# Attention scores computed with the keys on partitions, the maximum taken from the product of the high parts, and x normalised at the end

## The chip, the cores and the metric

One core of one Trainium2 chip runs the whole program. The metric is the device time in microseconds of one execution; shorter is better. The kernel before took 1103.06 us (median of three runs, 1101.69 to 1104.33).

## The reference

Attention in which a key counts for a query only if both fall into the same hash bucket, followed by a feed-forward layer with a squared ReLU. Everything is float32.

```python
batch, n_heads, seq, head_dim = (4, 8, 768, 64)       # B, H, S, D
n_tokens, d_model, d_ff = (3072, 512, 2048)
...
q_bits = (np.einsum('bhsd,dk->bhsk', q, proj) > 0)      # 6 bits; k_bits likewise
mask = q_bucket[:, :, :, None] == k_bucket[:, :, None, :]
scores = np.where(mask, (1 / np.sqrt(D)) * (q @ k.transpose(0, 1, 3, 2)), -1e9)
attn = np.exp(scores - scores.max(-1, keepdims=True))
attn = attn / (attn.sum(-1, keepdims=True) + 1e-9)
x = (attn @ v).transpose(0, 2, 1, 3).reshape(B * S, H * D)
r = np.maximum(x @ w_in, 0.0)
return (s * (r * r) + b) @ w_out
```

A query without any key in its bucket has equal scores everywhere, so its row of x is the mean of v.

## The kernel before

**Slots.** The work is cut into slots: 256 queries (`CH`) of one head of one batch, 96 in all. Batch 0 goes first with chunk 0 of its eight heads (slots 0 to 7), then the other two chunks of each head (8 to 23); the batches 1 to 3 follow with three chunks a head (24 to 95). Two neighbouring heads share a tile of x (64 partitions each), so the chunks of an odd head finish a pair.

**Precision.** A product of float32 numbers is made from fast `float32r` matmuls: an operand is split into a high part (rounded to `float32r`) and a low part (what is left). The first eight slots, and the values of some heads of batch 0 (`PLAIN`), use plain float32 matmuls, which take four passes.

**Scores** (`weights`, lines 467 to 503). Queries lie on partitions: for 128 queries two products (lines 483 and 484) add up scores and mask, 768 keys wide, in two banks of PSUM. The mask is part of the product: the bits stand as 12 more rows of the operands, times large constants. DVE takes the row maximum (491), ScalarE the exponential with the sum as a second output (492), DVE makes the inverse of the sum in four operations on one column (498 to 501), and POOL multiplies the 768 weights by it and puts equal weights into rows without a key (503).

**Values** (`values`, lines 508 to 571). The product with v needs the weights with keys on partitions, so PE transposes them (530), twelve 128 x 128 blocks a slot. ScalarE copies each group of four out of PSUM as the high part (541), DVE subtracts to get the low part (542), and PE multiplies both with v's two parts (551, 552). The result x is split again (568, 569) and written to HBM for the MoE.

**MoE** (`moe`, lines 578 to 641). It works on 256 tokens at a time, 12 units. For each pair of blocks of d_ff: 24 matmuls of 256 columns into bank 5 (605 to 607), ReLU, square and high part on ScalarE (611 to 613), the low part on POOL (614), and 12 matmuls of 512 columns into banks 6 and 7 (625 to 627). A unit can start once all eight heads of its chunk are done. The weights arrive in a coded form and are decoded in the first 260 us by ScalarE, DVE and POOL (`decode`, lines 281 to 313).

**Order.** Every step is entered into `Plan` with an engine, a cost, a priority and what it reads and writes; `Plan.order` (58) lays out a schedule by these costs, and the instructions are then issued in that order. Each engine works strictly in its order. Attention has the better priorities; MoE steps come where PE would otherwise be free by the plan's costs.

Of the kernel before, what the change touches and what calls it, by code (L numbers as in the profile page):

```python
# [20 lines left out]
FLOOR = -1.0e9  # L21
# [88 lines left out]
def lsh_attention_moe(ctx: ExitStack, tc, q, k, v, proj, w_in, w_out, s, b, out):  # L110
# [5 lines left out]
    HT = NT // 2  # L116
    HS = S // 2
# [51 lines left out]
    vn, vm = tile_("vn", [P, NT, D]), tile_("vm", [P, NT, D])  # L169
    VS = [tile_(f"vs{x}", [P, NT, 2, D], F32R) for x in range(2)]  # L170
# [16 lines left out]
    rb = tile_("rb", [P, 2, 2 * CH])
# [43 lines left out]
    crow = eb[0:1, 2, 0:2 * P].rearrange("o (p c) -> o p c", c=2)  # L231
    nc.vector.memset(eb[0:1, 2, 0:2 * P], 0.0)
# [7 lines left out]
    operands_p(F32)  # L240
# [106 lines left out]

    def prep(w, i, pr):
# [10 lines left out]
        def both(g, i, pr):  # L359

            pb = fill_bank(i)
            o = bank[:, pb, 0:HS]

            def tr():
                for t in range(HT):
                    nc.tensor.transpose(out=bank[:, pb, t * P:(t + 1) * P], in_=mk[:, g * HS + t * P:g * HS + (t + 1) * P], identity=ident)
            pe(0.33, tr, NK[g:g + 1], [("b", pb)], pr)
            to = (aq, EK[h])[g][0:D, 0:S].rearrange("d (t r n) -> d r t n", r=2, n=P)
            for r in range(2):
                act(HS, lambda r=r: nc.scalar.activation(to[:, r], o[r * D:(r + 1) * D].rearrange("d (t n) -> d t n", n=P), AF.Copy, scale=(SCALE, 1.0)[g]),  # L370
                    [("b", pb)], [("ks", x, r)] if g else AK(x, r=(0,), g=(r,)), pr)
            if g:
                ahead(pr)

        def split(g, i, pr):
            pb = fill_bank(i)
# [6 lines left out]
            act(HS, lambda: nc.scalar.activation(aq[:, cols], o, AF.Copy, scale=qk_sb), [("b", pb)], AK(x, g=(g,)), pr, 0.12)  # L383
            dve(HS, lambda: nc.vector.scalar_tensor_tensor(bq[:, cols], o, qk_sb, f32(aq[:, cols]), ALU.mult, ALU.subtract), [("b", pb)] + AK(x, g=(g,)), BK(x, g=(g,)), pr, 0.61)
            if g:
                dma(lambda: ks[0:D], lambda: aq[D:P].rearrange("p (o n) -> p o n", o=1).broadcast_to([D, 2, S]), AK(x, r=(1,)), [("ks", x, 0)], pr, 2 * D * S * 4)
                dma(lambda: ks[D:P, 0], lambda: bq[D:P], BK(x, r=(1,)), [("ks", x, 1)], pr, D * S * 4)

        def hash_(g, i, pr):
            pb = fill_bank(i)  # L390
            cols, o = slice(g * HS, (g + 1) * HS), bank[:, pb, 0:HS]

            if exact:
                def mx():
                    n = P if w < WARM else D
# [307 lines left out]
WARM = 3  # L703
# [30 lines left out]
```

## Time and profile before

| | |
|---|---|
| runs | 1101.69, 1103.06, 1104.33 us |
| profiled execution | span 1098.6 us from the first to the last instruction (4.5 us under the median; no time of its own is given for it) |
| TensorE clock granted | 0.995 of full speed on average |
| attention slots 24 to 95 | from about 250 us to about 890 us |
| MoE alone | from about 890 us to the end |
| POOL, normalising weights (line 503) | 193.4 us in 192 instructions |
| PE, transposes of weights (line 530) | 1152 instructions |

"Busy" counts the time in which an engine had an instruction running. Matmuls overlap, so the duration of one (0.28 us for 256 columns) is longer than the distance between two that follow each other; what PE needs is read from the distances.

### The profile page before, as it was taken

How to read it: one execution, taken by the hardware profiler on the slowest of the kernel's cores; microseconds unless marked ns; L12 is line 12 of the kernel's file. 1: busy time of each engine (PE TensorE's matmuls, PEld its weight loads, DVE VectorE, ACT ScalarE, POOL GpSimd, SP SyncE). 2: the span in 40 equal slices, each digit the busy share in tenths (PEclk: the TensorE clock that was granted, in tenths of full speed). 3: DMA queues.
4: the chain of work that ended last, by engine and by line, in shares of the span. 5: the costliest groups of instructions: out<-in, count | busy, mean ns of one | idle time of the engine just before them, and what ended most of it. 6: DMA issues, size and time to landing. Idle time of an engine off the chain costs nothing.

```text
span 1098.6 us, 19160 instructions
## 1 busy us (share of the span) xinstructions
PE 1067.2 (97%) x6950; PEld 940.7 (86%) x6950; DVE 666.6 (61%) x1577; ACT 671.2 (61%) x1321; POOL 473.2 (43%) x420
## 2 busy tenths in 40 slices
PE   7998887989999999999999999999999999999998
PEld 4455886768999999999999999999999999999997
DVE  4878789786677777777676777667767730000000
ACT  5887877876666666666666666666656643333332
POOL 4677867986333333343333333333333322222221
PEclk9999999999999999999999999999999999999999
DMA  6543334454233322432341343143223001101010
GB/s 185 175 132 112 103 87 120 127 142 132 74 80 90 107 63 74 130 86 60 94 113 42 78 116 94 48 118 92 74 59 113 20 30 58 39 20 58 1 39 20
DMA packets 79246, 93.53 MB, mean 85 GB/s; under 512 B 43824, under 2 KB 52016, under 8 KB 79152
## 3 DMA queue, kind: packets, MB, share of 16 engines
q1 hardware_dynamic: 73952, 75.26, 25.5%
q10 hardware_dynamic: 5200, 17.05, 4.9%
q8 instruction: 55, 0.90, 0.4%
q14 instruction: 39, 0.32, 0.1%
HBM read 49.03 MB, written 18.87 MB: 62 GB/s over the span
## 4 chain that ended last, share of the span: by engine, by line
PE 89%; DVE 4%; issue 2%; ACT 2%; POOL 2%; DMA 1%; POOLq 0%; ACTq 0%; DVEq 0%; SPq 0%
PE bank L530 11%; PE bank L605 8%; PE bank L606 8%; PE bank L607 8%; PE bank L625 8%; PE bank L627 8%; PE bank L626 8%; PE bank L483 5%; PE bank L484 5%; PE bank L552 5%; PE bank L551 5%; PE bank L549 3%; PE bank L481 1%; PE bank L381 1%; PE bank L407 1%
## 5 line engine op out<-in xcount | busy, mean ns | idle before, releaser
L503 POOL TENSOR_SCALAR eb<-eb,st 128x768 f32<-128x768 f32 x192 | 193.4, 1008 | 370.1 <-DVE st L501 225.8
L605 PE MATMUL bank<-xc,w 128*128 128x256 f32 x768 | 223.8, 291 | 1.8 <-ACT w L307 1.8
L491 DVE TENSOR_REDUCE st<-bank 128x1 f32<-128x768 f32 x192 | 183.4, 955 | 64.7 <-PE bank L484 53.9
L606 PE MATMUL bank<-xc,w 128*128 128x256 f32 x768 | 216.9, 282 | 2.0 <-POOL w L313 2.0
L607 PE MATMUL bank<-xc,w 128*128 128x256 f32 x768 | 216.4, 282 | 0.0
L614 POOL TENSOR_TENSOR glb<-rb,ghb 128x512 fp32r<-128x512 f32 x96 | 123.9, 1291 | 211.4 <-ACT ghb L613 158.5
L541 ACT CAST phdt.float32r<-bank 128x512 fp32r<-128x512 f32 x240 | 139.2, 584 | 113.1 <-PE bank L530 104.5
L542 DVE TENSOR_TENSOR plb<-bank,phdt.float32r 128x512 fp32r<-128x512 f32 x240 | 162.1, 684 | 48.0 <-ACT phdt.float32r L541 47.0
L492 ACT ACTIVATE eb<-bank,st 128x768 f32<-128x768 f32 x192 | 173.4, 903 | 26.8 <-DVE st L491 21.6
L530 PE MATMUL bank<-ident,eb 128*128 128x128 f32 x1152 | 168.1, 276 | 4.2 <-POOL eb L503 4.2
L625 PE MATMUL bank<-w,ghb 128*128 128x512 f32 x384 | 156.6, 408 | 0.0
L530 PEld LDWEIGHTS bank<-ident,eb 128*128 128x128 f32 x1152 | 134.3, 142 | 22.4 <-issue 11.2
L626 PE MATMUL bank<-w,ghb 128*128 128x512 f32 x384 | 151.7, 395 | 0.0
L627 PE MATMUL bank<-w,glb 128*128 128x512 f32 x384 | 151.3, 394 | 0.2 <-POOL glb L614 0.2
L605 PEld LDWEIGHTS bank<-xc,w 128*128 128x128 f32 x768 | 145.8, 190 | 6.0 <-ACT w L307 2.1
L606 PEld LDWEIGHTS bank<-xc,w 128*128 128x128 f32 x768 | 146.1, 190 | 5.0 <-POOL w L313 2.2
L607 PEld LDWEIGHTS bank<-xc,w 128*128 128x128 f32 x768 | 145.9, 190 | 0.0
L611 ACT ACTIVATE rb<-bank 128x512 f32<-128x512 f32 x96 | 57.4, 598 | 144.4 <-PE bank L607 143.8
L552 PE MATMUL bank<-plb,vs 128*128 128x256 f32 x480 | 125.7, 285 | 6.1 <-DVE plb L542 6.0
L551 PE MATMUL bank<-phdt.float32r,vs 128*128 128x256 f32 x480 | 128.3, 289 | 0.5 <-ACT phdt.float32r L541 0.5
L483 PE MATMUL bank<-ks,aq 128*128 128x384 f32 x352 | 125.0, 355 | 2.8 <-ACT eb L492 2.8
L484 PE MATMUL bank<-ks,bq 76*128 76x384 f32 x352 | 120.1, 341 | 0.0
(100 smaller groups left out, 1715.8 us busy)
## 6 DMA issues: line engine op xcount, KB each, us to landing
xd<-xsb SPq DMA_DIRECT2D x48, 256.0 KB
xc<-xd SPq DMA_DIRECT2D x48, 256.0 KB
ks<-aq SPq DMA_DIRECT2D x24, 384.0 KB
raw<-in_moe_w_in_dram ACTq DMA_DIRECT2D x16, 512.0 KB
raw<-in_moe_w_out_dram ACTq DMA_DIRECT2D x16, 512.0 KB
nat<-in_q_dram SPq DMA_DIRECT2D x32, 192.0 KB
nat<-in_k_dram SPq DMA_DIRECT2D x32, 192.0 KB
aq<-aq SPq DMA_DIRECT2D x32, 192.0 KB
```

The lines of the kernel that those rows point to most:

```text
L483: nc.tensor.matmul(o, aq[:, ts], ks[:, 0, cols], start=True, stop=False)
L491: dve(S, lambda: nc.vector.tensor_reduce(nm, sc, AX.XY, ALU.max, negate=True), bk, [("st", y, 0)], pr, 0.95)
L503: pool(S, lambda: nc.gpsimd.tensor_scalar(e, e, rz, u, ALU.mult, ALU.add), [("st", y, 2)], [ek], pr, 1.01)
L530: nc.tensor.transpose(out=bank[:, tb, o:o + P], in_=eb[:, es[a], kt * P:(kt + 1) * P], identity=ident)
L551: nc.tensor.matmul(av, vs[:, kt], PH[0][:, y, m], start=(kt == 0), stop=False)
L552: nc.tensor.matmul(av, vs[:, kt], plb[:, y, m], start=False, stop=(kt == NT - 1))
L605: nc.tensor.matmul(hp, w[:, 0, fs], xc[:, 0, :], start=(cc == 0), stop=False)
L606: nc.tensor.matmul(hp, w[:, 1, fs], xc[:, 0, :], start=False, stop=False)
L607: nc.tensor.matmul(hp, w[:, 0, fs], xc[:, 1, :], start=False, stop=(cc == NC_ - 1))
L625: nc.tensor.matmul(o, gh[:, ts], w[:, 0], start=(f == 0), stop=False)
L626: nc.tensor.matmul(o, gh[:, ts], w[:, 1], start=False, stop=False)
L627: nc.tensor.matmul(o, gl[:, ts], w[:, 0], start=False, stop=(f == NF - 1))
```

## The change

- The scores are computed with keys on partitions (`scores`): for each 128 keys and 256 queries a *lead* product (high part of k times high part of q, with the mask's rows) and a *rest* product (the low parts) into the same place. Six of each fill three banks, two key blocks a bank. There is one such set of banks, 0 to 2, for all slots.
- The maximum is taken from the lead products alone: DVE reduces over the six key blocks (output 128 x 256), PE transposes that, DVE reduces over the partitions' 128, PE transposes the result back, and DVE writes the negated maxima as two rows of an operand (one for each 128 queries). These rows enter with the rest product, against rows of ones, so that ScalarE's exponential needs no bias and writes weights with keys on partitions.
- The weights are therefore no longer transposed. ScalarE makes the high part from SBUF, POOL subtracts for the low part.
- The sum over keys: DVE adds the six blocks of weights (five additions of 256 columns), ScalarE and DVE split the result, and two matmuls with a matrix of ones sum over partitions and spread it over all of them. Where the values are plain float32, a column of ones beside v gives the sum instead.
- x is normalised at the end, for a pair of heads at once: threshold for empty rows, reciprocal, product, and addition of v's mean, on 256 columns each.
- `PLAIN` takes all eight heads of batch 0; preparing goes in three pieces of 256 columns instead of two of 384; the exact bits need one product instead of two; a MoE group's matmuls are entered one by one.

```diff
-    def weights(i, a, pr):
...
-        dve(S, lambda: nc.vector.tensor_reduce(nm, sc, AX.XY, ALU.max, negate=True), bk, [("st", y, 0)], pr, 0.95)
-        act(S, lambda: nc.scalar.activation(e.rearrange("p (g n) -> p g n", g=2), sc, AF.Exp, bias=nm, accum_out=z),
-            bk + [("st", y, 0)], [ek, ("st", y, 1)], pr, 0.28)
...
-        pool(S, lambda: nc.gpsimd.tensor_scalar(e, e, rz, u, ALU.mult, ALU.add), [("st", y, 2)], [ek], pr, 1.01)
+    def scores(i, pr):
...
+                    nc.tensor.matmul(o, ks[0:HR + TPC, 0, kt], aq[0:HR + TPC, cs], start=m == 0, stop=m == 1, skip_group_check=True)
...
+        sc = bank[:, b0:b0 + NP_].rearrange("p b (m n) -> p n b m", n=CH)
+        dve(S * TPC, lambda: nc.vector.tensor_reduce(t, sc, AX.XY, ALU.max), [("b", b) for b in pb], [tk], pr, 1.75)
...
+                nc.tensor.transpose(out=bank[:, 4, j * P:(j + 1) * P], in_=t[:, j * P:(j + 1) * P], identity=ident)
...
+        dve(CH, lambda: nc.vector.tensor_reduce(nm, bank[:, 4, 0:CH].rearrange("p (j n) -> p j n", j=TPC), AX.X, ALU.max, negate=True), [("b", 4, 0)], [nk], pr, 0.4)
...
+        pe(0.115, lambda: nc.tensor.transpose(out=bank[0:TPC, 4, 0:P], in_=nm, identity=ident), [nk], [("b", 4, 0)], pr)
...
+            nc.vector.scalar_tensor_tensor(mr.rearrange("p (j n) -> p j n", j=TPC), o, -FLOOR, d, ALU.min, ALU.mult)
+        dve(CH, rows, [("b", 4, 0)], [mk], pr, 0.36)
...
+                    nc.tensor.matmul(o, ks[:, 1, kt], bq[:, cs], start=False, stop=m == 1, skip_group_check=True)
...
+            act(512, lambda p=p, z=z: nc.scalar.activation(et(z), bank[:, pb[p]], AF.Exp), [("b", pb[p])], [ek(z)], pr + EP)
...
+    def values(i, pr, pieces):
...
-                        nc.tensor.transpose(out=bank[:, tb, o:o + P], in_=eb[:, es[a], kt * P:(kt + 1) * P], identity=ident)
...
+                act(512, lambda z=z, y=y: nc.scalar.copy(HL[2 * y], E[z]), [("e", z)], [("hl", 2 * y)], pr)
+                pool(512, lambda z=z, y=y: nc.gpsimd.tensor_tensor(HL[2 * y + 1], E[z], f32(HL[2 * y]), ALU.subtract), [("e", z), ("hl", 2 * y)], [("hl", 2 * y + 1)], pr, 1.3)
...
+                    dve(CH, lambda z=z, m=m, a=ZB if p else E[z][:, 0:CH]: nc.vector.tensor_tensor(ZB, a, E[z][:, m * CH:(m + 1) * CH], ALU.add), [("e", z)], ["zb"], pr, 0.35)
...
+            act(CH, lambda: nc.scalar.copy(zhl[:, 0], ZB), ["zb"], ["zh"], pr)
+            dve(CH, lambda: nc.vector.scalar_tensor_tensor(zhl[:, 1], ZB, EPS / P, f32(zhl[:, 0]), ALU.add, ALU.subtract), ["zb", "zh"], ["zl"], pr, 0.4)
...
+                    nc.tensor.matmul(zz, oner, zhl[:, j], start=(j == 0), stop=(j == 1))
...
+            dve(CH, lambda: nc.vector.tensor_scalar(ub, zp, 1e-6, vmn[:, n:n + 1], ALU.is_lt, ALU.mult), zk + [("vm", n, 0), ("vm", n, 1)], ["ub"], pr, 0.35)
+            dve(CH, lambda: nc.vector.reciprocal(zp, zp), [], zk, pr, 0.35)
+            dve(CH, lambda: nc.vector.tensor_tensor(t, t, zp, ALU.mult), zk, xk, pr, 0.35)
+            dve(CH, lambda: nc.vector.tensor_tensor(t, t, ub, ALU.add), ["ub"], xk, pr, 0.35)
...
-PLAIN = (4, 5, 6, 7)
+ODD = ()
+FB = (5, 6, 7)
 WP = -8
-MP = 0.0
+EP = -4
+PLAIN = (0, 1, 2, 3, 4, 5, 6, 7)
+MP = 1e4
```

What this does to DVE's order, in batch 1. Before, the stretch from one 768-wide maximum (L491) to the next, with the second half of the work on one 128-query tile (L542 is the low part of the transposed weights, L498 to L501 the inverse of the sum):

```order
L491 TENSOR_REDUCE st<-bank 128x1
L542 TENSOR_TENSOR plb<-bank,phdt.float32r_2326 128x512 x2
L498 TENSOR_SCALAR st<-st 128x1
L499 TENSOR_SCALAR st<-st 128x1
L500 RECIPROCAL st<-st 128x1
L501 TENSOR_SCALAR st<-st 128x1
L564 TENSOR_TENSOR xpb<-xpb,bank 64x256
L491 TENSOR_REDUCE st<-bank 128x1
```

Of the changed kernel (its own line numbers), DVE from the wide maximum (L527) of a slot, where a pair is also being finished (`zb` is the running sum, `e` the weights, `zpb` the sums of both heads, `ub` the threshold, `nmt` the maxima, `bq` the operand that gets the two rows):

```order
L527 TENSOR_REDUCE mx<-bank 128x256
L622 TENSOR_SCALAR ub<-zpb,vmn 128x256
L579 TENSOR_TENSOR zb<-e_91 128x256
L623 RECIPROCAL zpb<-zpb 128x256
L533 TENSOR_REDUCE nmt<-bank 128x2
L624 TENSOR_TENSOR xpb<-xpb,zpb 128x256
L579 TENSOR_TENSOR zb<-zb,e_92 128x256
L625 TENSOR_TENSOR xpb<-xpb,ub 128x256
L541 SCALAR_TENSOR_TENSOR bq_70<-bank,ident 2x256
```

Between the wide maximum and the two rows (L541) now stand the reciprocal and the pair's other operations, and additions of the slot ahead. The next rows of the same order, up to the following wide maximum:

```order
L579 TENSOR_TENSOR zb<-zb,e_92 128x256
L627 TENSOR_TENSOR xsb<-xpb,xsb 128x256
L579 TENSOR_TENSOR zb<-zb,e_93 128x256
L617 TENSOR_TENSOR xpb<-xpb,bank 64x256
L579 TENSOR_TENSOR zb<-zb,e_93 128x256
L387 SCALAR_TENSOR_TENSOR bq_70<-bank,misc,aq_68 128x256
L485 TENSOR_REDUCE vp<-vn 128x64
L687 SCALAR_TENSOR_TENSOR osb<-bank,misc,bcs 128x512
L608 SCALAR_TENSOR_TENSOR zhl<-zb,zhl 128x256
L527 TENSOR_REDUCE mx<-bank 128x256
```

The low part of the sum (L608) has moved in directly ahead of the next wide maximum. ScalarE's order in batch 1, from the three exponentials of one slot (L558) on (`hl` are the high parts of the weights):

```order
L558 ACTIVATE e_91<-bank 128x512
L558 ACTIVATE e_92<-bank 128x512
L558 ACTIVATE e_93<-bank 128x512
L607 CAST zhl<-zb 128x256
L615 COPY xpb<-bank 64x256
L481 CAST vs_4979<-vn 128x6x64
L575 CAST hl_1928<-e_91 128x512
L614 ACTIVATE zpb<-bank 64x256
L575 CAST hl_1940<-e_92 128x512
L575 CAST hl_2012<-e_93 128x512
L386 ACTIVATE aq_68<-bank,misc 128x256
```

The high part of the sum (L607), which L608 on DVE waits for, stands behind the third exponential of the slot that follows. Per slot PE's order has, in place of twelve transposes, three small ones (L531 twice, L535 once), and behind its last attention matmul stand 864 MoE matmuls of 256 columns and 446 of 512, where before 828 and 432 stood.

More of the change, by code (lines that the diff above doesn't have):

```diff
@@ L359, in both @@
         def both(g, i, pr):
[L361 to L376, printed above, removed]
+            pb = fill_bank()
             cols, o = slice(g * HS, (g + 1) * HS), bank[:, pb, 0:HS]
@@ L436, in keys @@
[L436 to L441 removed]
+            act(S, lambda: nc.scalar.copy(ks[0:D, 0], k_[0:D]), KK(e), KK(x, (0,)), pr)
+            dma(lambda: ks[TPC:D, 1], lambda: ks[TPC:D, 0], KK(x, (0,)), KK(x, (3,)), pr, D * S * 4)
@@ new lines, in sums, with new @@
+            def sums():
+                for t in range(NT):
+                    nc.tensor.matmul(bank[0:D, 4, CH:CH + 1], values_at(h, t)[:, 0:D], ones, start=(t == 0), stop=(t == NT - 1))
+            pe(0.8, sums, vk, [("b", 4, 1)], pr)
+            mean(bb, h, pr)
+            return
+        y, sk = w % 2, [("vs", w % 2, 0), ("vs", w % 2, 1)]
+        plain = not bb and h in PLAIN
+        def new():
+            VS[y] = wk.tile([P, NT, 2, D], F32 if plain else F32R, tag=f"vs{y}", name=f"vs{w}")
@@ new lines, in prep_values, with plain, et, ek @@
+        pe(0.25, lambda: nc.tensor.matmul(bank[0:D, 4, CH:CH + 1], vp, ones, start=True, stop=True), ["vp"], [("b", 4, 1)], pr)
+        mean(bb, h, pr)
+    def plain(i):
+        return not slots[i][0] and (i < EARLY or slots[i][1] in PLAIN)
+    def et(z):
+        return E[z] if z < NE else HL[z - NE]
+    def ek(z):
+        return ("e", z) if z < NE else ("hl", z - NE)
+    def halves():
+        for x in range(2 * NHL):
+            def new(x=x):
+                HL[x] = wk.tile([P, 2 * CH], F32R, tag=f"hl{x}", name=f"hl{x}")
+            plan.add(None, 0.0, new, [], [("hl", x)], 0)
@@ L673, in lsh_attention_moe @@
             parts = prep(w + 2, i, pr) if w + 2 in preps else resplit(w + 2, i, pr) if visits[w + 2]["x"] in (0, 1) else []
-        for a in range(TPC):
-            weights(i, a, pr + WP)
+        if not i:
+            ahead = scores(0, WP)
+            next(ahead), next(ahead, None)
+        if i + 1 < NSL:
+            ahead = scores(i + 1, pr + 10 + WP)
+            next(ahead)
         if nd[0] >= ND:
@@ L685, in lsh_attention_moe @@
         values(i, pr + 5, now)
+        if i + 1 < NSL and plain(i) and not plain(i + 1):
+            halves()
+        next(ahead, None)
         if last and w + 2 < len(visits):
```

346 lines of the change are left out of this document (185 added, 161 removed).

## The prediction

> **What bounds the kernel now.** I read the page's totals and its 40 slices first, then the chain that ended last, then the busy time of each engine by stretches (start and end, length, then PE, PEld, DVE, ACT, POOL, the granted clock and the DMA).
>
> ```profile
> PE 1067.2 (97%) x6950; PEld 940.7 (86%) x6950; DVE 666.6 (61%) x1577; ACT 671.2 (61%) x1321; POOL 473.2 (43%) x420
> ```
> ```profile
> PE   7998887989999999999999999999999999999998
> ...
> DVE  4878789786677777777676777667767730000000
> ...
> POOL 4677867986333333343333333333333322222221
> ```
> ```profile
> PE 89%; DVE 4%; issue 2%; ACT 2%; POOL 2%; DMA 1%; POOLq 0%; ACTq 0%; DVEq 0%; SPq 0%
> ```
> ```profile
> 100.00:150.00 50.00, 43.93 (x273) 38.42 (x272) 41.77 (x84) 39.15 (x78) 41.80 (x35) 0.93 0.36 104
> ...
> 200.00:250.00 50.00, 47.20 (x260) 33.74 (x259) 39.96 (x80) 37.27 (x75) 44.73 (x36) 1.00 0.51 149
> ...
> 400.00:500.00 100.00, 100.00 (x709) 94.37 (x708) 75.00 (x187) 66.21 (x135) 37.20 (x35) 1.00 0.35 89
> ...
> 900.00:1000.00 100.00, 100.00 (x639) 90.52 (x638) 2.90 (x4) 32.97 (x54) 21.85 (x18) 1.00 0.11 36
> ```
> Three stages. Up to about 250 us (batch 0, weights being decoded) all engines wait for one another; from 250 to 880 us PE is full and DVE idles a quarter of the time; after that PE alone runs what is left of the MoE. Where PE is full, a slot (256 queries of one head) takes what PE has to do in it. In the timeline, the first maximum of slot 24 and that of slot 95 give the pace (start, duration):
>
> ```profile
> 249.60 0.94 DVE L491 TENSOR_REDUCE st<-bank 128x1 f32<-128x768 f32 x1
> ...
> 879.35 0.96 DVE L491 TENSOR_REDUCE st<-bank 128x1 f32<-128x768 f32 x1
> ```
> (879.35 - 249.60) / 71 = **8.87 us a slot**. The stage has 72 slots, so a tenth of a microsecond per slot is 7.2 us of the total.
>
> **What PE is spared.** Starts of neighbouring matmuls in the timeline, and a run of transposes in the chain, give the unit prices: 0.12 us for 256 columns, 0.23 for 512, 0.11 for a transpose.
>
> ```profile
> 507.58 0.28 PE L605 MATMUL bank<-xc,w 128*128 128x256 f32 x1
> 507.70 0.28 PE L606 MATMUL bank<-xc,w 128*128 128x256 f32 x1
> ...
> 503.55 0.39 PE L626 MATMUL bank<-w,ghb 128*128 128x512 f32 x1
> 503.78 0.39 PE L627 MATMUL bank<-w,glb 128*128 128x512 f32 x1
> ...
> 480.62 0.88 PE bank L530 x8
> ```
> Per slot go 12 transposes (1.32 us). The scores cost the same (8 x 384 columns before, 12 x 256 now), so do the values. New are 3 small transposes (0.33) and 2 matmuls for the sums (0.24). Net -0.75. The order puts a little less MoE into slots 24 to 71 (811 short and 408 long matmuls for 843 and 423): -0.15 a slot. PE's own pace would be 8.87 - 0.9 = **8.0 us**. The order fixes how much MoE stands in a slot, so if another engine needs longer, PE waits, and nothing fills that wait.
>
> **What a slot now costs on the way round.** Only one set of score banks is left (0, 1, 2), so slots follow each other in a closed chain: exponentials, lead products, wide maximum, maximum across, rows, rest products, exponentials. In it DVE works in order, with the pieces of the sum and of the normalising between. Prices, from the groups by line (busy us, mean ns; for L569 shortest, median and longest in ns):
>
> ```profile
> L491 DVE TENSOR_REDUCE st<-bank 128x1 f32<-128x768 f32 x192 | 183.4, 955 | 64.7 <-PE bank L484 53.9
> ...
> L542 DVE TENSOR_TENSOR plb<-bank,phdt.float32r 128x512 fp32r<-128x512 f32 x240 | 162.1, 684 | 48.0 <-ACT phdt.float32r L541 47.0
> ...
> L564 DVE TENSOR_TENSOR xpb<-xpb,bank 64x256 f32<-64x256 f32 x80 | 33.9, 424 | 30.3 <-ACT xpb L562 28.9
> ...
> L569 DVE TENSOR_TENSOR xsb<-xpb,xsb x48: 407/425/1529, 48.0 to 896.5; 128x256 fp32r<-128x256 f32 x48
> ...
> L412 DVE TENSOR_SCALAR nat<-bank,misc 44x384 f32<-44x384 f32 x48 | 31.9, 665 | 6.0 <-PE bank L409 5.4
> ...
> L541 ACT CAST phdt.float32r<-bank 128x512 fp32r<-128x512 f32 x240 | 139.2, 584 | 113.1 <-PE bank L530 104.5
> ...
> L568 ACT CAST xsb<-xpb 128x256 fp32r<-128x256 f32 x48 | 19.3, 403 | 10.3 <-DVE xpb L564 10.0
> ...
> L501 DVE TENSOR_SCALAR st<-st 128x1 f32<-128x1 f32 x192 | 41.1, 214 | 6.7
> ```
> From 256 to 512 columns out of PSUM adds 0.26 us, 1.0 ns a column; the wide maximum over 1536 columns is then 0.955 + 768 x 1.0 = 1.73 us. An operation on 256 columns is 0.42 (a PSUM operand) or 0.43 (two SBUF operands); 256 columns of preparing 0.5; an exponential over 512 columns 0.59; the threshold for empty rows (one SBUF operand) 0.21 to 0.43, taken 0.35.
>
> From the end of a slot's third exponential:
> 1. ScalarE's high part of the sum 0.40, then DVE's low part 0.43 and the addition to x 0.42, which stand ahead of the wide maximum in DVE's order: 1.3 with the hand-overs. The lead products are ready before that.
> 2. Wide maximum 1.73: 3.0.
> 3. DVE to the rows. Without a pair to finish (even heads): add, preparing, maximum across, add, preparing, rows = 2.7. With a pair (odd heads): threshold 0.35, add 0.43, reciprocal, maximum across 0.42, product, add, add 3 x 0.43, rows 0.42 = 2.9 + reciprocal. PE's transposes lie beside.
> 4. First rest products 0.4, three exponentials 1.77, hand-overs 0.3: 2.5.
>
> **The reciprocal** of 256 columns is in no row; one column is (shortest, median, longest).
>
> ```profile
> L500 DVE RECIPROCAL st<-st x192: 155/164/167, 20.9 to 885.8; 128x1 f32<-128x1 f32 x192
> ...
> L498 DVE TENSOR_SCALAR st<-st x192: 132/154/157, 20.7 to 885.6; 128x1 f32<-128x1 f32 x192
> ```
> It takes 10 ns longer than the addition beside it (medians). If that is a fixed cost, 256 columns are some 0.3 to 0.4 us; if every column costs it, 0.16 + 256 x 0.010 = 2.7. A plain pass should not differ by 10 ns on a single column, so I lean to the upper end and take 2.2.
>
> The Trainium skill, "VectorE: DVE Perf Modes", section "First, the fixed hardware budget", says that the reciprocal is an iterative divide with a repeat count of 8; an estimate by it is 256 x 8 / 0.96 GHz = 2.1 us, and the sum below would stay within 7 us of itself. A reciprocal at one column a cycle would make it about 1117. The one-column row fits the first reading, and no run here shows it at 256.
>
> **Waits between DVE and POOL.** In the timeline, a DVE instruction with two SBUF operands outlasts all that POOL has queued; the other rows are of the groups:
>
> ```profile
> 136.74 3.64 DVE L436 TENSOR_TENSOR ks<-ek,ks 64x768 fp32r<-64x768 f32 x1
> ...
> 137.02 1.30 POOL L313 TENSOR_TENSOR w<-osb,w 128x512 fp32r<-128x512 f32 x1
> 138.27 1.30 POOL L312 TENSOR_TENSOR bcs<-bcs,osb 128x512 f32<-128x512 f32 x1
> ...
> L304 DVE SCALAR_TENSOR_TENSOR osb<-osb,raw x32: 675/1308/3417, 28.5 to 259.1; 128x512 int32<-128x512 int32 x32
> ...
> L569 DVE TENSOR_TENSOR xsb<-xpb,xsb 128x256 fp32r<-128x256 f32 x36 | 17.4, 485 | 1.7 <-ACT xsb L568 1.3
> ...
> L614 POOL TENSOR_TENSOR glb<-rb,ghb 128x512 fp32r<-128x512 f32 x96 | 123.9, 1291 | 211.4 <-ACT ghb L613 158.5
> ```
> It ends at 140.38, 0.8 us behind the second POOL row. Where POOL is busy 84 to 89% of the time (the windows at 100 and 200 us), L304 takes 0.63 us more than its shortest; where POOL is busy 37%, L569 (its 36 between 300 and 900 us) takes 0.06 more than its median. Per slot the change gives POOL three subtractions of 512 columns (3 x 1.29), 0.9 of the MoE's and 0.35 of the values': 5.1 us, 51% of a 10 us slot. Between the two measured ends that is 0.2 us for each such DVE operation. DVE gets 7.5 of them a slot instead of 0.5; about three lie on the way from sum to rows: **0.6 us a slot** (bounds 0.2 and 1.9).
>
> The Trainium skill, "SBUF — State Buffer", section "SBUF: two separate sides", has the pair of ports as an exclusive lock held for a whole instruction; this trace agrees (136.74 above). By that rule an operation finds POOL at work in 51% of cases and waits half of 1.29 us, an estimate of 0.33 each, 1.0 a slot, and the sum would be about 1210.
>
> **The sum.** Even heads 1.3 + 1.7 + 2.7 + 2.5 = 8.2; odd heads 1.3 + 1.7 + 5.1 + 2.5 = 10.6; mean 9.4, with the waits **10.0**. That is above PE's 8.0, so DVE sets the pace and PE waits 2 us a slot.
> - Slots 24 to 95: 72 x (10.0 - 8.87) = +81.
> - Behind the last attention matmul stand 864 short and 446 long MoE matmuls instead of 828 and 432: +36 x 0.12 + 14 x 0.23 = +7.5.
> - Slots 0 to 23: PE loses 280 transposes (-31) and half the exact bit products (-11), gains 72 small transposes (+8), the exact slots' row products (+6), four-pass values in eight slots more (+13) and sums (+9); no normalising on POOL is left there, but the exact slots lose their second set of banks. -10, between -30 and +15.
>
> 1098.6 - 10 + 81 + 7.5 = 1177 of span. The span is 4.5 us under the median of the runs shown (1103.06); added back, **1182 us**.
>
> **Rivals.** *PE keeps the pace (faster):* DVE's additions find POOL idle and the reciprocal is one plain pass, so that a slot's chain stays below 8.87 us, the point from which it decides. At PE's 8.0: 1098.6 - 10 - 63 + 7.5 + 4.5 = 1038; at 8.7 (odd heads 1.9 us shorter, waits 0.2), 1088. For it: PE is the bound today and 45 us of transposes go from that stage. Against: the low part of the sum stands ahead of the wide maximum, and eight operations in odd slots between maximum and rows. *Only the reciprocal is cheap:* 8.5 + 0.6 = 9.1 a slot, 1117. *POOL's run of three goes first:* if DVE's additions wait for all three subtractions (from 1.4 to 5.3 us, 2.3 behind the maximum), a slot takes 11.7, some 1305.
>
> **Chances.** Forecast (1135 to 1240) 0.58; cheap reciprocal with waits (1090 to 1135) 0.18, of which 0.02 and 0.03 end faster or level; PE's pace (under 1090) 0.16; over 1240, 0.08. So faster by over 0.2% 0.18, within it 0.03, slower 0.79 (0.2%, about 2 us, is what a measurement of this kernel can tell). The range 1080 to 1240 leaves out some 2 in 10.
>
> **What would show it.** Right: PE 85 to 90% busy with idle time behind the rows and the exponentials; the wide maximum near 1.7 us, 10 us apart; the reciprocal near 2 us; the additions' mean well over 0.43; a tail of some 210 us in which PE is full. Wrong: PE full from 250 us on, or a wide maximum every 8 us; a reciprocal of 0.3 to 0.4 us; additions at 0.43 throughout, or a strided wide maximum far over 1.7 us.

## The result and the profile after

The changed kernel takes **1238.8 us** (median of four runs, 1236.9 to 1241.6), the kernel before in the same session 1103.2 (1101.7 to 1104.3): 1.124 times as long, 95% interval 1.122 to 1.126. The forecast was 1182 us, in a range of 1080 to 1240: the median lies 1.2 us inside its upper bound, and two of the four runs (1240.25 and 1241.6) lie above it.

The totals of the page after, its 40 slices (PE, DVE, POOL) and the shares of the chain that ended last:

```profile
PE 1081.4 (87%) x6862; PEld 934.5 (75%) x6862; DVE 864.6 (70%) x1367; ACT 680.5 (55%) x1377; POOL 567.9 (46%) x441
...
PE   8888798789888888898889788888888899999998
...
DVE  6566679778888998988889889888888882000000
...
POOL 3245466465454545454555454454445452222222
...
PE 40%; DVE 28%; issue 5%; ACT 4%; DMA 1%; POOL 0%; SPq 0%; DVEq 0%; ACTq 0%; POOLq 0%
```

PE has lost its row of nines except in the tail; DVE has won eights and nines, and its share of the chain rose from 4 to 28%. The first wide maximum of slot 24 and the one of slot 95, in the timeline:

```profile
273.55 1.75 DVE L527 TENSOR_REDUCE mx<-bank 128x256 f32<-128x1536 f32 x1
...
1010.08 1.76 DVE L527 TENSOR_REDUCE mx<-bank 128x256 f32<-128x1536 f32 x1
```

(1010.08 - 273.55) / 71 = **10.37 us a slot**, against 8.87. The lost time therefore lies in three places:

| stretch | before | after | difference |
|---|---|---|---|
| start to slot 24 | 249.6 | 273.6 | +24.0 |
| slot 24 to slot 95 | 629.8 | 736.5 | +106.8 |
| slot 95 to the end of the span | 219.3 | 228.4 | +9.2 |
| span | 1098.6 | 1238.5 | +139.9 |

One slot of the middle stretch, DVE alone (start, duration, line, operation; in brackets what it stood idle for):

```profile
405.87 1.76 DVE L527 TENSOR_REDUCE mx<-bank 128x256 f32<-128x1536 f32 x1
407.55 0.44 DVE L624 TENSOR_TENSOR xpb<-xpb,zpb 128x256 f32<-128x256 f32 x1
407.91 1.51 DVE L579 TENSOR_TENSOR zb<-zb,e 128x256 f32<-128x256 f32 x1
409.35 0.41 DVE L625 TENSOR_TENSOR xpb<-xpb,ub 128x256 f32<-128x256 f32 x1
409.69 0.41 DVE L533 TENSOR_REDUCE nmt<-bank 128x2 f32<-128x256 f32 x1
...
411.50 0.41 DVE L541 SCALAR_TENSOR_TENSOR bq<-bank,ident 2x256 fp32r<-2x256 f32 x1 [0.62 <-PE bank L411]
...
414.73 0.43 DVE L608 SCALAR_TENSOR_TENSOR zhl<-zb,zhl 128x256 fp32r<-128x256 f32 x1 [0.29 <-ACT zhl L607]
415.18 0.42 DVE L617 TENSOR_TENSOR xpb<-xpb,bank 64x256 f32<-64x256 f32 x1
415.64 1.76 DVE L527 TENSOR_REDUCE mx<-bank 128x256 f32<-128x1536 f32 x1
```

Between the wide maximum (405.87) and the maximum across (409.69) stand three pieces of other work, and one, an addition of 256 columns, takes 1.51 us instead of 0.42. The groups by line, and for single lines of the view of tiles the shortest, median and longest in ns:

```profile
L527 DVE TENSOR_REDUCE mx<-bank 128x256 f32<-128x1536 f32 x96 | 168.6, 1756 | 40.9 <-PE bank L522 15.8 <-PE bank L520 13.8 <-ACT osb L304 7.0
L579 DVE TENSOR_TENSOR zb<-zb,e 128x256 f32<-128x256 f32 x288 | 167.1, 580 | 5.9
L623 DVE RECIPROCAL zpb<-zpb 128x256 f32<-128x256 f32 x48 | 83.8, 1746 | 0.7
L624 DVE TENSOR_TENSOR xpb<-xpb,zpb 128x256 f32<-128x256 f32 x48 | 38.5, 802 | 0.2
L535 PE MATMUL bank<-ident,nmt 128*2 128x128 f32 x96 | 27.1, 283 | 71.3 <-DVE nmt L533 49.7
...
L617 DVE TENSOR_TENSOR xpb<-xpb,bank x72: 422/424/427, 291.7 to 1027.6; 64x256 f32<-64x256 f32 x72
L579 DVE TENSOR_TENSOR zb<-zb,e x288: 401/424/1523, 284.0 to 1020.8; 128x256 f32<-128x256 f32 x144
L624 DVE TENSOR_TENSOR xpb<-xpb,zpb x48: 398/658/2062, 59.5 to 1028.1; 128x256 f32<-128x256 f32 x48
```

L617 has an operand in PSUM: all 72 take 0.42 us. L579 and L624 have the same width and two operands in SBUF: they take 0.40 at the least and up to 2 us. The mean of L579 is 0.16 above its median. The timelines of DVE and POOL, laid side by side, show where that comes from: 201 of the 288 additions start while POOL runs nothing; they take 0.415 us in the mean and 0.428 at most. The other 87 start while POOL is at work and take 0.96. L617 takes 0.42 in either case. PE's idle time stands behind the same stretch of DVE's order: ahead of L535, which transposes the result of DVE's maximum across (L533), it waits for 71.3 us in all, 49.7 of them until L533 is done.

### The profile page after: what moved, and what is told of

It reads as the page before. It is cut to its first block, busy times and chain, and to the rows that moved or that the text cites. A ratio compares the mean times of both kernels' runs of the same rounds, so it can differ in the third digit from the quotient of the medians.

```text
span 1238.5 us, 19203 instructions
## 1 busy us (share of the span) xinstructions
PE 1081.4 (87%) x6862; PEld 934.5 (75%) x6862; DVE 864.6 (70%) x1367; ACT 680.5 (55%) x1377; POOL 567.9 (46%) x441
## 4 chain that ended last, share of the span: by engine, by line
PE 40%; DVE 28%; issue 5%; ACT 4%; DMA 1%; POOL 0%; SPq 0%; DVEq 0%; ACTq 0%; POOLq 0%
PE bank L662 13%; PE bank L679 12%; DVE mx L527 8%; DVE zb L579 5%; DVE zpb L623 5%; PE bank L552 4%; PE bank L522 2%; DVE xpb L624 2%; PE bank L586 2%; PE bank L587 2%; DVE nmt L533 2%; DVE ub L622 1%; DVE nat L414 1%; DMA vn<-in_v_dram 1%; ACT e L558 1%
## 5 line engine op out<-in xcount | busy, mean ns | idle before, releaser
L576 POOL TENSOR_TENSOR hl<-e,hl 128x512 fp32r<-128x512 f32 x216 | 283.3, 1339 | 245.9 <-ACT hl L575 173.5
L662 PE MATMUL bank<-xc,w 128*128 128x256 f32 x2304 | 351.4, 289 | 1.4 <-ACT rb L667 1.1
L662 PEld LDWEIGHTS bank<-xc,w 128*128 128x128 f32 x2304 | 311.5, 192 | 11.9 <-ACT rb L667 2.9
L527 DVE TENSOR_REDUCE mx<-bank 128x256 f32<-128x1536 f32 x96 | 168.6, 1756 | 40.9 <-PE bank L522 15.8
L579 DVE TENSOR_TENSOR zb<-zb,e 128x256 f32<-128x256 f32 x288 | 167.1, 580 | 5.9
L558 ACT ACTIVATE e<-bank 128x512 f32<-128x512 f32 x240 | 127.9, 598 | 59.8 <-PE bank L552 49.8
L679 PEld LDWEIGHTS bank<-w,ghb 128*128 128x128 f32 x768 | 138.9, 192 | 17.2 <-DVE osb L687 1.1
L586 PE MATMUL bank<-hl,vs 128*128 128x256 f32 x432 | 123.2, 301 | 1.0 <-DVE xpb L617 1.0
L575 ACT CAST hl<-e 128x512 fp32r<-128x512 f32 x216 | 122.5, 621 | 0.8
L587 PE MATMUL bank<-hl,vs 128*128 128x256 f32 x432 | 117.4, 287 | 0.3 <-POOL hl L576 0.2
L535 PE MATMUL bank<-ident,nmt 128*2 128x128 f32 x96 | 27.1, 283 | 71.3 <-DVE nmt L533 49.7
L586 PEld LDWEIGHTS bank<-hl,vs 128*128 128x128 f32 x432 | 84.3, 195 | 4.3 <-ACT ghb L669 1.3
L587 PEld LDWEIGHTS bank<-hl,vs 128*128 128x128 f32 x432 | 84.5, 195 | 4.0 <-POOL hl L576 0.7
```

The lines of the kernel that those rows point to most:

```text
L527: dve(S * TPC, lambda: nc.vector.tensor_reduce(t, sc, AX.XY, ALU.max), [("b", b) for b in pb], [tk], pr, 1.75)
L558: act(512, lambda p=p, z=z: nc.scalar.activation(et(z), bank[:, pb[p]], AF.Exp), [("b", pb[p])], [ek(z)], pr + EP)
L575: act(512, lambda z=z, y=y: nc.scalar.copy(HL[2 * y], E[z]), [("e", z)], [("hl", 2 * y)], pr)
L576: pool(512, lambda z=z, y=y: nc.gpsimd.tensor_tensor(HL[2 * y + 1], E[z], f32(HL[2 * y]), ALU.subtract), [("e", z), ("hl", 2 * y)], [("hl" ...
L579: dve(CH, lambda z=z, m=m, a=ZB if p else E[z][:, 0:CH]: nc.vector.tensor_tensor(ZB, a, E[z][:, m * CH:(m + 1) * CH], ALU.add), [("e", z)] ...
L586: nc.tensor.matmul(av, VS[w % 2][:, kt], HL[2 * y][:, ms], start=(kt == 0), stop=False)
```

## The experiments

All pairs of kernels below share a chip with the kernel before, which took 1100.6 to 1104.7 us beside them. Each ran once, so differences of a few microseconds in the total say little. First the numbers, from the timelines (first wide maximum of a slot) and the results:

| kernel | slot 8 | slot 24 | slot 95 | us a slot, 24 to 95 | total |
|---|---|---|---|---|---|
| after | 121.7 | 273.6 | 1010.1 | 10.37 | 1238.8 |
| e1 small reciprocal | 121.0 | 265.9 | 973.2 | 9.96 | 1204.3 |
| e2 small POOL work | 124.8 | 276.2 | 955.2 | 9.56 | 1182.6 |
| e3 small additions | 123.1 | 274.2 | 982.1 | 9.97 | 1213.1 |
| e4 true costs in the plan | 117.3 | 269.0 | 1067.1 | 11.24 | 1223.9 |
| e5 = e1 + e2 + e3 | 120.0 | 263.0 | 898.2 | 8.95 | 1124.9 |
| e6 early load held back | 110.0 | 262.3 | 997.4 | 10.35 | 1229.8 |
| e7 sum not split | 120.8 | 275.2 | 998.8 | 10.19 | 1255.1 |
| e8 = e6, e7, wide additions | 109.9 | 264.1 | 954.9 | 9.73 | 1236.4 |
| e9 = e5, third of the maximum | 114.7 | 258.5 | 890.8 | 8.91 | 1117.5 |
| e10 = e8, true costs | 107.6 | 262.0 | 952.7 | 9.73 | 1194.8 |
| e11 = e6, second bank set | 109.1 | 268.8 | 1009.2 | 10.43 | 1241.6 |
| e12 = e6, tall lead products | 109.2 | 261.8 | 996.7 | 10.35 | 1229.1 |

**e1: the reciprocal on 8 columns of 256.**

```diff
-nc.vector.reciprocal(zp, zp)
+nc.vector.reciprocal(zp[:, 0:8], zp[:, 0:8])
```

> The reciprocal is computed on 8 of its 256 columns; the rest of x is left without the division. The order on every engine is that of the changed kernel. Theory (what DVE has in its order between the wide maximum and the rows sets the slot): the reciprocal took 1.75 us, 48 times, 36 of them in slots 24 to 95, so 58 to 77 us go: 1160 to 1180. Rival (the closed chain over one set of banks sets the slot, DVE has slack in it): under 15 us, 1224 or more.

The result, 1204.3, lies between the two. The reciprocal falls from 1.75 to 0.20 us, 0.78 a slot (one for two slots); 0.41 comes off the slot. The groups of e1 show where a part went:

```profile
L624 DVE TENSOR_TENSOR xpb<-xpb,zpb 128x256 f32<-128x256 f32 x48 | 46.6, 972 | 0.2
L625 DVE TENSOR_TENSOR xpb<-xpb,ub 128x256 f32<-128x256 f32 x48 | 45.0, 937 | 0.3
```

L624 took 802 ns before the edit, L625 555: DVE reaches them sooner, while POOL is still at work, and waits there. In the timelines, 28 of the 48 L625 start while POOL runs an instruction; before the edit it was 8.

**e2: POOL's subtraction on 8 columns of 512;** the product with the low part uses the high part.

```diff
-nc.gpsimd.tensor_tensor(HL[2 * y + 1], E[z], f32(HL[2 * y]), ALU.subtract)
+nc.gpsimd.tensor_tensor(HL[2 * y + 1][:, 0:8], E[z][:, 0:8], f32(HL[2 * y])[:, 0:8], ALU.subtract)
...
-nc.tensor.matmul(av, VS[w % 2][:, kt], HL[2 * y + 1][:, ms], ...)
+nc.tensor.matmul(av, VS[w % 2][:, kt], HL[2 * y][:, ms], ...)
```

> POOL's subtraction for the low part of the weights works on 8 of 512 columns, and the product of the low part multiplies the high part again, so x lacks the low part. Theory (DVE operations with two SBUF operands wait until POOL's instruction ends): the additions fall from 0.58 to about 0.43 us on average, 0.6 to 1.2 us a slot, 1150 to 1195. Rival (DVE's own work is the bound and the waits fall where it would wait anyway): under 20 us, 1218 or more.

The theory holds. It is the largest single gain: 0.81 us a slot, 56 of the total, and not one DVE instruction was touched. Busy time from 400 to 500 us (length, PE, PEld, DVE, ACT, POOL, clock, DMA), after and in e2, then the additions in e2, and PE's idle time behind the maximum across, after and in e2 (us in all, times, longest):

```profile
400.00:500.00 100.00, 85.88 (x599) 75.51 (x598) 91.13 (x148) 61.72 (x131) 51.62 (x41) 1.00 0.28 71
...
400.00:500.00 100.00, 90.86 (x637) 80.48 (x636) 85.17 (x154) 65.96 (x141) 20.53 (x44) 1.00 0.30 75
...
L579 DVE TENSOR_TENSOR zb<-zb,e 128x256 f32<-128x256 f32 x288 | 129.3, 449 | 5.9
...
PE bank L535 <- DVE nmt L533: 49.7, 34, 5.5
...
PE bank L535 <- DVE nmt L533: 23.0, 23, 7.1
```

With POOL busy 21% instead of 52%, an addition takes 0.45 in the mean instead of 0.58 (the first of a slot 0.43 instead of 0.65), which makes the five of a slot 0.74 us shorter. PE's waiting for the subtraction's result can't be the cause; in the kernel after it comes to less than 1 us in all:

```profile
L587 PE MATMUL bank<-hl,vs 128*128 128x256 f32 x432 | 117.4, 287 | 0.3 <-POOL hl L576 0.2
...
L587 PEld LDWEIGHTS bank<-hl,vs 128*128 128x128 f32 x432 | 84.5, 195 | 4.0 <-POOL hl L576 0.7
```

**e3: the five additions of the sum on 8 columns each.**

```diff
-nc.vector.tensor_tensor(ZB, a, E[z][:, m * CH:(m + 1) * CH], ALU.add)
+nc.vector.tensor_tensor(ZB[:, 0:8], a[:, 0:8], E[z][:, m * CH:m * CH + 8], ALU.add)
```

> The five additions for the sum over keys work on 8 of 256 columns, so the sum is incomplete. Theory (DVE sets the slot): 360 additions of 0.59 us shrink to about 0.1; of five a slot about three stand on the way from the maximum to the rows or ahead of the next maximum: 1.5 to 2.4 us a slot, 1065 to 1130, not below what PE needs (8.0 us a slot). Rival (the chain of maximum, transposes, exponentials alone needs the 10.4 us): under 30 us, 1208 or more.

The rival's number comes out (26 us), but not for its reason: in e2 the same chain ran at 9.56 us a slot. An addition of 8 columns still takes 0.37 us with POOL busy, and 0.25 in e5, where POOL is quiet:

```profile
L580 DVE TENSOR_TENSOR zb<-zb,e 128x8 f32<-128x8 f32 x288 | 106.2, 369 | 9.9 <-ACT e L559 5.9
...
L580 DVE TENSOR_TENSOR zb<-zb,e 128x8 f32<-128x8 f32 x288 | 71.1, 247 | 9.8 <-ACT e L559 5.8
```

**e5: e1, e2 and e3 together.** The edits are those above.

> The three cuts of the first runs together: reciprocal and additions on 8 columns, POOL's subtraction on 8 columns with the high part in the place of the low part (x lacks division, sum and low part). Order on PE as in the changed kernel. Theory (DVE's work and its waits for POOL set the slot): alone the cuts took 0.41, 0.81 and 0.40 us off a slot of 10.37; without POOL's instructions the time cut from DVE can't come back as waits, so together at least their sum, 8.0 to 8.75 a slot, span 1070 to 1125. Rival (the closed chain of maximum, transposes, rows and exponentials over one set of banks needs more than that by itself): 9.2 or more a slot, 1150 or more.

8.95 us a slot lies between the two forecasts, the total at the upper end of the theory's. The single gains add up to 1.62, together they give 1.42, so they are not "at least their sum". The total is still above that of the kernel before, though most of DVE's new load is gone. **e9** asks whether DVE or PE sets this pace:

```diff
-sc = bank[:, b0:b0 + NP_].rearrange("p b (m n) -> p n b m", n=CH)
+sc = bank[:, b0:b0 + 1].rearrange("p b (m n) -> p n b m", n=CH)
...
-nc.scalar.activation(et(z), bank[:, pb[p]], AF.Exp)
+nc.scalar.activation(et(z), bank[:, pb[p]], AF.Exp, scale=0.0)
```

> The kernel e5_all (small reciprocal, small additions, small subtraction on POOL) with one thing more: the wide maximum reads only the first of the three score banks (512 of 1536 elements per partition), and the exponentials have scale 0, so that all weights are 1. It leaves out two thirds of the maximum and the scores' effect on the weights. The wide maximum should fall from 1.76 to about 0.8 us, so DVE's chain loses 1 us a slot. Theory: in e5_all PE paces (95 to 98% busy, 8.95 us a slot), so the slots come out at 8.4 to 8.9, total 1085 to 1122. Rival: DVE's chain still paces e5_all, then the whole microsecond comes off: 8.0 or less a slot, total 1060 or less.

The theory holds: the wide maximum loses 1.07 us, the slot 0.04. The same window in e5 and e9, and the maximum in e9:

```profile
400.00:500.00 100.00, 96.05 (x673) 85.83 (x673) 72.63 (x170) 70.47 (x151) 21.98 (x47) 1.00 0.34 87
...
400.00:500.00 100.00, 96.57 (x680) 86.70 (x679) 61.66 (x173) 70.31 (x150) 24.08 (x46) 1.00 0.36 91
...
L528 DVE TENSOR_REDUCE mx<-bank 128x256 f32<-128x512 f32 x96 | 66.1, 688 | 14.5 <-PE bank L523 8.1 <-PE bank L521 2.6 <-ACT ex L559 2.2
```

DVE drops from 73 to 62% and PE stays at 96%: DVE's work no longer sets the pace. What PE needs by itself shows in the distances between PE's starts in the timeline, added up by line over 300 to 880 us (us a slot):

| PE's work | before | e9 |
|---|---|---|
| transposes of weights (12) | 1.14 | 0 |
| scores | 1.47 | 1.55 |
| values | 1.48 | 1.65 |
| MoE, short and long | 4.27 | 4.36 |
| preparing | 0.50 | 0.60 |
| small transposes and sums | 0 | 0.43 |
| waits | 0 | 0.32 |
| sum | 8.87 | 8.91 |

PE now has 8.6 us of work in a slot of 8.9. In the kernel after the same account gives 8.91 of work and 1.46 of waits, in e2 8.70 and 0.86.

**e4: the plan is told what DVE's operations really take.**

```diff
-... ["zb"], pr, 0.35)
+... ["zb"], pr, 0.6)
...
-nc.vector.reciprocal(zp, zp), [], zk, pr, 0.35)
+nc.vector.reciprocal(zp, zp), [], zk, pr, 1.75)
```

(low part 0.52, threshold 0.6, product 0.7, addition of the mean 0.55.)

> The same instructions; only the costs that the plan is told are those measured (additions 0.6, reciprocal 1.75, the pair's other operations 0.55 to 0.7, low part of the sum 0.52), so the order changes: 536 short and 288 long MoE matmuls stand behind the last attention matmul instead of 864 and 446. Theory (DVE paces the slots at 10.4 us and PE's waits stayed empty because the plan did not know of them): the tail shrinks by 328 x 0.12 + 158 x 0.23 = 75 us, the slots stay near 10.4 us: 1150 to 1180. Rival (PE's waits can't be filled, since they come where PE stands behind a result): slots grow by as much as the tail shrinks, 1225 to 1250.

The total is just under the rival's range: the tail shrinks from 228 us to 155, and the slots take 62 us more. PE now waits for the MoE's input, and the clock falls around such waits (waits of PE by line; a window):

```profile
PE bank L662 <- DMA xc<-xd: 13.4, 4, 4.5
...
610.00:620.00 10.00, 6.17 (x24) 5.58 (x25) 4.01 (x7) 3.25 (x7) 3.85 (x3) 0.66 0.46 140
```

The account of PE's starts shows what the longer slot holds (us a slot, 300 to 880 us, against the kernel after): 0.94 more of MoE (5.43 for 4.49), 0.52 more for the same work beside it (4.94 for 4.42), and only 0.59 less waiting (0.87 for 1.46). From 300 to 850 us the granted clock is 0.93, for 0.98 after; that this is the whole cause of the 0.52 was not tested. That an order by true costs needn't do so shows in e10.

**e7: the sum over keys not split;** one product of plain float32 (four passes) with ones in place of high and low part, and two buffers for the sum.

```diff
-act(CH, lambda: nc.scalar.copy(zhl[:, 0], ZB), ["zb"], ["zh"], pr)
-dve(CH, lambda: nc.vector.scalar_tensor_tensor(zhl[:, 1], ZB, ...), ["zb", "zh"], ["zl"], pr, 0.4)
...
+pe(mmc(CH, 4), lambda: nc.tensor.matmul(zz, ones.broadcast_to([P, P]), ZB, start=True, stop=True), [zbk], zk, pr + 3)
```

> The sum over keys is not split: one four-pass float32 matmul with ones takes it as it is (a second buffer for it), so ScalarE's high part and DVE's low part of the sum are gone, which stood ahead of every wide maximum. The plan then expects faster slots and leaves more MoE: 973 short and 456 long matmuls behind the last attention matmul instead of 864 and 446, some 15 us. Theory (what stands ahead of the wide maximum in DVE's order is on the chain): 0.6 to 1.0 us a slot less, 43 to 72 us, total 1180 to 1212. Rival (lead products come no earlier, the low part was hidden): slots within 0.2 us of 10.37, total 1235 to 1255.

The rival's numbers come out, the total at its upper end: 0.18 a slot, and the total gets longer, because the plan puts less MoE into the slots (behind the last product with v stand 973 short and 504 long matmuls in its timeline, in that of the kernel after 864 and 446). The 456 long ones in the text are 48 too few; with 504 the tail should grow by 109 x 0.12 + 58 x 0.23 = 26 us and not by 15, and it does (254.6 for 228.4). **e8** adds e6 and makes two additions of 512 columns and a product over both halves out of five additions:

```diff
-dve(CH, lambda z=z, m=m, a=...: nc.vector.tensor_tensor(ZB, a, E[z][:, m * CH:(m + 1) * CH], ALU.add), ...)
+dve(2 * CH, lambda z=z, a=ZB if p > 1 else E[PIECES[i][0]]: nc.vector.tensor_tensor(ZB, a, E[z], ALU.add), ...)
```

> The load held back and the unsplit sum, and besides the sum over keys by two additions of 512 columns instead of five of 256 (one buffer; two four-pass matmuls). 1080 short and 515 long MoE matmuls are left for the end: +41 us there. Theory: DVE operations that can wait for POOL fall from 6 to 2 a slot; slots 24 to 95 lose 1.2 to 1.8 us (86 to 130 us), the front 15 to 25: 1125 to 1180. Rival (each wait for POOL just grows with fewer of them): slots not under 9.4, total 1200 or more.

The rival's number again: 9.73 a slot, and a still longer tail (1080 and 563; 51 us, since the 515 of the text is 48 too low as well). Its reason does not show. The two wide additions take 0.70 and 0.85 us in the mean, with medians of 0.69: 0.01 and 0.16 of waiting, where a narrow one has 0.16 to 0.22. What DVE does instead is stand idle ahead of the first of them, for the most part until PE's sum over keys (L608) is done, which reads the single buffer:

```profile
L578 DVE TENSOR_TENSOR zb<-e,e 128x512 f32<-128x512 f32 x72 | 50.2, 697 | 63.5 <-PE bank L608 35.6 <-ACT xpb L611 17.4 <-ACT e L557 10.4
```

Whether a second buffer would shorten the slots was not tested. **e10** is e8 with the true costs (wide addition 0.85, the others as in e4):

> Nothing is left out: e8_wide (early load held back, unsplit sum, additions of 512 columns) with the measured costs of DVE's operations told to the plan, so that it puts more MoE into the slots. Theory: PE waits 1 us a slot in e8_wide (9.73), and MoE put there is free; the tail falls from 1080 short and 515 long matmuls to 912 and 431, which is 168 x 0.12 + 84 x 0.23 = 39 us, and the slots stay under 10.0: total 1195 to 1220. Rival, as in e4_costs: the MoE put into the slots delays DVE's chain as much as the tail gains; slots 10.2 or more, total 1225 or more.

The counts of long matmuls in this text, 515 and 431, are each 48 too low; in the timelines the tail goes from 1080 and 563 to 912 and 479, so the differences and the 39 us stand. The theory holds, and the total, 1194.8, is at its lower end: the tail gains its 39 us and the slots lose nothing. By the account of starts, PE's waits fall from 1.02 to 0.55 us a slot and its work rises by as much, from 8.70 to 9.16. The window shows PE at 96% beside a busy POOL:

```profile
400.00:500.00 100.00, 95.76 (x646) 84.16 (x645) 75.55 (x115) 60.96 (x127) 53.93 (x41) 1.00 0.30 78
```

It computes all that the reference does, is 44 us shorter than the changed kernel, and 94 longer than the one before.

**e6: the front.** After slot 1, DVE stands idle for a load, and PE for DVE (timeline, first DVE, then PE); the windows after that are those of the changed kernel and the one before:

```profile
48.48 0.80 DVE L485 TENSOR_REDUCE vp<-vn 128x64 f32<-128x384 f32 x1 [5.66 <-DMA vn<-in_v_dram]
...
49.66 0.37 PE L535 MATMUL bank<-ident,nmt 128*2 128x128 f32 x1 [5.54 <-DVE nmt L533]
...
50.00:60.00 10.00, 10.00 (x35) 6.36 (x35) 6.20 (x10) 4.22 (x8) 2.54 (x2) 0.50 0.17 52
...
50.00:60.00 10.00, 10.00 (x45) 5.07 (x43) 8.96 (x18) 8.54 (x17) 6.58 (x6) 1.00 0.62 197
```

The sum over v is for batch 1, which comes 220 us later; the plan had put it some 70 instructions into DVE's order, and the load lands only at about 48 us. Behind the gap the granted clock is 0.50. In e6 that load waits until the x of the first odd head is done:

```diff
-plan.add(SP, 0.7, lambda: nc.sync.dma_start(to, vd), [], ["vn"], pr, 0.9)
+plan.add(SP, 0.7, lambda: nc.sync.dma_start(to, vd), [("xp", 0, 1)] if w == 2 * H else [], ["vn"], pr, 0.9)
```

> Nothing is computed otherwise; the first load of v for batch 1 has to wait for the x written last before it in the program, so that the sum over v (the operation on vn) leaves its place among the first 70 of DVE's order and stands behind slot 12. Theory (the first eight slots lost 20 us because DVE waited 5.7 us at 43 us for that load, PE stood still and its clock was halved for some 10 us twice): slots 0 to 7 take 10.7 to 11.5 us instead of 13.2, total 1212 to 1226. Rival (the single set of banks and the row products make the first slots long): under 5 us, 1234 or more.

The result lies between the two forecasts. Slot 8 comes 11.8 us earlier, slot 24 11.3, the total 9: about half of the front's 24. From 50 to 60 us the granted clock is now 0.98. Slots 0 to 7 still take 11.7 us each. **e11** gives three of the early slots banks of their own (`ODD = (1, 3, 5)`), **e12** makes all their lead products 128 rows tall (`WARM = 8` instead of 3):

> Nothing is left out: e6_vn (early load held back) with a second set of score banks for half of the first eight slots (ODD = (1, 3, 5)), so that an early slot's lead products need not wait for the exponentials of the slot before. Theory: what is left of the loss in the first eight slots (11.71 us a slot against 10.7 before the change) is the single set of banks; then slots 0 to 7 fall by 0.7 to 1.3 us each, total 1220 to 1225. Rival: what is left is DVE's and POOL's load there (decoding, preparing, sums), then slots 0 to 7 stay at 11.5 to 11.9 and the total at 1227 to 1233.

> Nothing is left out: e6_vn (early load held back) with the lead products of all eight early slots 128 rows tall instead of 76 from the fourth on (the added rows of k are zeros). In e6_vn the granted clock stands at 0.50 from 85 to 90 us and at 0.60 to 0.72 up to 105 us although PE is busy nearly throughout; what it runs there is matmuls of 1 and 2 rows, then twelve of 76 rows, at twice their usual time. Theory: the clock follows how many rows are at work, and with tall lead products it comes back at once: mean clock over 50 to 110 us above 0.95, slots 3 to 7 about 1 us shorter each, total 1220 to 1226. Rival: the clock falls in the gaps and the short matmuls and the height of the lead products changes nothing: clock over 50 to 110 us 0.80 to 0.88, total 1227 to 1233.

In e11 the banks 5 to 7 also serve preparing, which writes between the two products of these three slots, so their scores are not the reference's; the work is the same. Slots 0 to 7 take 11.49, a hair below the rival's 11.5: banks of their own, as given here, don't bring back what is left. The total, 1241.6, is longer than either forecast: slots 8 to 23 take 7 us more than in e6, and those behind them 5. Since the three slots share their banks with preparing, the run doesn't clear the single set for good. In e12 the rival's numbers come out. The clock comes back sooner once, but the total stays (windows of e6 and e12):

```profile
90.00:100.00 10.00, 9.32 (x34) 6.27 (x33) 7.09 (x9) 3.97 (x9) 3.95 (x3) 0.67 0.29 102
...
90.00:100.00 10.00, 9.18 (x47) 6.33 (x45) 8.77 (x11) 3.93 (x8) 5.46 (x4) 1.00 0.29 99
```

In the next ten microseconds it is lower than in e6, 0.68 against 0.80. From 50 to 110 us the mean is 0.86 against 0.83 in e6, far from the theory's 0.95, and slot 8 moves by 0.8 us. What costs the other half of the front stays open.

## Why the prediction was right in the main, and where its terms were off

**The sign, and DVE as the pace: right.** The pace was put at 10.0, it is 10.37; the stage was to cost 81 us, it costs 107. e2, e1 and e9 show the mechanism: with POOL's or DVE's work cut the slots shrink at once, and once PE is at 96% nothing more comes off.

**The time: inside the range by luck.** The three stretches were to add 78.5 us to the span; they add 139.9. Of the 61 missing, the front makes 34, the slots 26, the tail 2. The range reached just far enough, and the largest miss is a term outside these slots.

**The waits between DVE and POOL: right, and in sum a little small.** The forecast was 0.2 us for an operation with two SBUF operands; the additions show 0.16 in the mean. Three such waits, 0.6 a slot, were put on the path; taking most of POOL's work away gives 0.81, so more than three of them cost the slot time. The rival in which additions wait for all three of POOL's subtractions (1305 us) doesn't appear: the longest addition takes 1.52 us. The sentence on the rule of the exclusive ports (the Trainium skill, "SBUF — State Buffer", section "SBUF: two separate sides") said 1.0. The trace agrees with the rule's kind: L617 with its PSUM operand never outlasts 0.427 us. The size is off because fewer additions meet POOL than its share of the time suggests, 87 of 288 or 30% instead of 51%; those that do lose 0.55 us each.

**The reciprocal: right in kind, 2.2 us against 1.75.** Every column costs, and the rival of a cheap pass is gone. The sum had slots in which a pair is finished 2.4 us longer than others, and that is what the timeline shows: from one wide maximum to the next it takes 11.66 us where one reciprocal starts in between (25 cases) and 9.26 where none does (41; in 5 cases there are two). But with the reciprocal made small the slot doesn't get the whole of it back: of 0.78 a slot, e1 returned 0.41. There the first kind falls to 10.15 and the second rises to 9.75. The rival *only the reciprocal is cheap* put the total at 1117; e1 makes it cheap and takes 1204.

**Step 1, the low part ahead of the wide maximum: by e7 mostly not on the path.** It was priced at 1.3 us, 0.83 of it for the two splitting operations; e7 takes these two away and gains 0.18. That bounds their price from neither side, since in e7 the order differs, PE's sum is heavier, and the clock is 0.95 from 400 to 500 us.

**The wide maximum: right,** 1.73 against 1.756: a read across six key blocks costs no more per element than one along the row.

**The sum of the chain was therefore close partly by offsetting errors.** It has too much for the reciprocal and, by e7, for step 1, and too little for how tightly DVE is filled: from 300 to 850 us it is busy 489.0 of 550 us, 9.2 a slot, so there is little slack, and a late operand or a wait for POOL can delay the next maximum from places other than the steps counted. That this makes up the difference is argued, not shown.

**PE's own pace: wrong, 8.0 forecast, 8.6 of work and slots of 8.9 measured in e9.** The step was the net sparing of 0.75 and 0.15 us a slot. The account above shows 12 transposes at 0.09 (1.14, not 1.32), 0.43 for the new small ones and the sums (not 0.57), 0.35 more for scores and values, which were taken as equal, and preparing, which was not counted. The MoE's matmuls are a little fewer, as counted, but each takes a little longer, 0.09 more in all instead of 0.15 less. The work falls by 0.28, and that goes into waits. So the first rival, "PE keeps the pace" at 1038 to 1088 us, didn't come about even with a small reciprocal and POOL at 21%: e5 shows 1125. The forecast's time didn't rest on this term, since DVE was slower; the chance of 0.16 for the rival did.

**The front: wrong, -10 forecast, +24 measured,** outside its own bounds of -30 to +15. The work on PE was counted, not the order on DVE. e6 ties about half to a load that stands too early in DVE's order and to the half clock behind that wait; the other half has no cause shown.

**The tail: right,** +7.5 against +9.2.

## What to carry to other kernels

When work moves from POOL's one pass and PE to many short passes on DVE, add up the DVE's whole slot and look for POOL work beside it: 256 columns on two SBUF operands cost 0.42 us alone and 0.58 beside a POOL that is half busy, and narrower operands help little there (8 columns, 0.37). Before counting what an engine is spared, make the account of everything that stays on it, from distances between starts: PE was spared 0.28 us a slot, not 0.9. In a planned order, an instruction that isn't urgent but stands early can stall its engine for its load.

## What was not expected of the hardware

One gap of 5.5 us on PE (44 to 49.7 us) is followed by a granted clock of 0.50 from 48 to 62 us, though PE is busy without a break from 50 us on. The Trainium skill, "TensorE: Matmul & The Clock Gate", section "Part 1: The HAM clock gate (the "warmup" mystery)", has the clock fall after about 3.4 us of idling, which fits a gap of this length, and return after about 3.4 us of sustained work, which does not: here it took some 14 us. What ran there were mostly products with one column and matmuls of 1, 2 and 76 rows. Shorter gaps are followed by a fall too: in e6, one of 2.36 us (to 81.1 us) by a clock of 0.50 from 85 to 90 us. In e12 all the lead products with 76 rows have 128. Two slots' lead products in its timeline:

```profile
84.04 5.49 PE L520 MATMUL bank<-eq,ek 128*128 128x256 f32 x12
...
94.85 2.86 PE L520 MATMUL bank<-eq,ek 128*128 128x256 f32 x12
```

The first twelve take twice the time of the second: tall matmuls don't prevent the fall, but the window from 90 us on has its clock back, which in e6 it had not. Behind the next gap (2.27 us, to 102.1 us) the clock falls again, so whether the height matters stays open.

A reciprocal of 256 columns takes 1.746 us in the mean of 48, 6.2 ns for each column beyond the first (0.164 us for one): four times the price of an addition of that width.
